# A long convolution and its gradient on one core: from an 8-point-by-channel spectrum with complex products to real products on 4-channel blocks summed in PSUM

## The chip, the core and the metric

The kernel runs on one core of one Trainium2 chip. The metric is the device time of one execution in microseconds. The core's engines have short names in the profile: PE is TensorE's matmul, PEld its weight load, DVE is VectorE, ACT is ScalarE, POOL is GpSimd, SP is SyncE, which here only issues DMAs.

## The reference: what is computed

One block is run forward and backward. The block has two branches on the layernorm of A_q (2,048 tokens by 512 channels, bf16): a gated MLP, and a product with a causal convolution over the whole sequence, which the reference computes by real FFTs of length 4,096.

```
xn = layernorm(A_q)
kv = shift4(A_k) * A_v                       # a 4-tap causal filter, then v
y  = irfft(rfft(kv, 4096) * rfft(ssm_k, 4096))[:2048] + kv * ssm_D
s  = xn * y
g  = silu( (sigmoid(xn @ w_gate) * (xn @ w_up)) @ w_down )
out = A_q + s * g
```

The kernel returns `out` and the gradients of a scalar through it with respect to q, k, v, the shift filter, ssm_k (512 by 2,048), ssm_D and the three MLP weights. The gradient of the convolution needs the spectrum of the gradient dy, and two products of it with a conjugated spectrum: with K's for d(kv), and with kv's for d(ssm_k). Both are transformed back.

## The kernel before: how the work is staged

**Recording and planning.** The kernel doesn't write its instructions in the order in which they run. All of them are recorded in `Rec` (`add`, L234), with their dependencies by region of SBUF or PSUM bank. Generators (strK, strV, strX and so on) are interleaved by `run_streams` (L497), by how much TensorE work each has yielded. `Rec.order` (L337) then plays the list through with a cost for each instruction (`cost` L283, `dcost` L312 for DMAs) and decides in which order each engine gets its instructions, which PSUM bank a tile has, and, for an evacuation recorded by `evac` (L231), whether ScalarE or VectorE does it. `emit` (L487) writes them in this order, so that every compute instruction in the profile stands at L493. An engine takes its instructions strictly in that order, and so does each DMA queue: what waits holds up what is behind it.

**PSUM.** Eight banks are given out by kind (L175): three pairs ("mm2") for the transforms in the first part and two pairs ("mm2c") in the last, two single banks for accumulations ("acc") and two for transposes ("tr"). A matmul group can begin only when a bank of its kind has been evacuated.

**Stage A, to about 182 us: the forward convolution, with part of the MLP beside it.** The 512 channels go in four groups (cg) of 128. The sequence of 2,048 is 128 by 16 (token = 16 p + j). For each group and each of K (the convolution kernel), V (that is, kv) and later C (dy):

- `step1` (L833): 32 matmuls against the cosine and sine tables Cf, one for each j and for real and imaginary part, give Q; four evacuations of 1,024 columns.
- `flip` (L844): 32 transposes, so that the 16 values of j come onto the partitions; four evacuations. A block has 8 channels: 16 j by 8 channels are 128 partitions, and real and imaginary part are separate blocks.
- `step3` (L853), four times a group (qq): the 16-point factor on j. As real and imaginary input are separate blocks, a complex result takes four matmuls of 512 columns, two each into the real and the imaginary half; one evacuation.
- `cmul` (L864): the complex product on VectorE, two multiplications of 1,024 columns and two sums of 512.
- `inv3` (L872): back from the product, eight matmuls of 256 columns (four blocks, each with real and imaginary part), one evacuation.
- `inv1` (L881): the inverse of step1.

`strK` (L892) and `strV` (L914) bring K and V to the flipped form, `strX` (L947) runs step3 for K and V, stores both spectra to HBM as `KK_d` (by POOL's queue) and does the product and the inverse. Beside them runs strG, the MLP's forward pass for ten of the sixteen token blocks (`f_gen`, L687), which has three sigmoids a block on ScalarE. At the very start `gen_fft_consts` (L523) makes the tables: integer angles on VectorE, sines on ScalarE, then BD (the 16-point factor, used by step3) and R (its inverse, used by inv3). The transposes of strK (L900) read their columns with a step of 16 elements.

**Stage B, about 182 to 336 us.** The rest of the MLP forward and its backward, block by block (`stepB`, L1113), with activations transposed by DMA on SP's queue and stored.

**Stage C, from about 336 us: the convolution's gradient beside the weight gradients.** `dW` (L1169) multiplies stored activations, which SP's queue loads (`ld_L`, L1158), into the three weight gradients. Beside it, `frontC` (L1207) brings dy to the flipped form and `backC` (L1229) runs, for each quarter qq of a group: step3, two complex products with the stored spectra (loaded by `ld_KK`, L1201, on POOL's queue into a ring of two), and two inv3, one for each product. The rest of backC gives d(k), d(v), the shift filter's gradient and d(ssm_k). When it has ended, the last weight gradients run alone.

Of the kernel before, what the change touches and what calls it, by code (L numbers as in the profile page):

```python
# [16 lines left out]
P = 128  # L17
# [6 lines left out]
NJ = 16  # L24
# [13 lines left out]
FBS = [(0, 4), (4, 4), (8, 3)]  # L38

# [129 lines left out]
class Rec:  # L169
# [142 lines left out]
    def dcost(self, alt):  # L312
# [17 lines left out]
        rate = 360e3 if run >= 2048 else 300e3 if run >= 1024 else 250e3 if run >= 512 else 150e3 if run >= 256 else run * 500  # L330
# [192 lines left out]
def gen_fft_consts(nc, ar, a, b, negpi, Cf, BD, R):  # L523
# [10 lines left out]
    pa = tmp([1], i32)  # L534
    nc.vector.tensor_single_scalar(pa, pi_, 3, ALU.arith_shift_right)
    pe = tmp([1], i32)
    nc.vector.tensor_single_scalar(pe, pi_, 7, ALU.bitwise_and)
    paf = tmp([1], f32)
    nc.vector.tensor_copy(paf, pa)
    pef = tmp([1], f32)  # L540
    nc.vector.tensor_copy(pef, pe)
    cb = tmp([16, 8], f32)
    nc.gpsimd.iota(cb, pattern=[[1, 16], [0, 8]], base=0, channel_multiplier=0, allow_small_or_imprecise_dtypes=True)
    ce = tmp([16, 8], f32)
    nc.gpsimd.iota(ce, pattern=[[0, 16], [1, 8]], base=0, channel_multiplier=0, allow_small_or_imprecise_dtypes=True)
    ab = tmp([16, 8], i32)
    nc.vector.tensor_scalar(ab, cb, paf[:, 0:1], None, ALU.mult)
    mask = tmp([16, 8], f32)
    nc.vector.tensor_scalar(mask, ce, pef[:, 0:1], None, ALU.is_equal)
    ang = tmp([3, 16, 8], i32)  # L550
    nc.vector.tensor_single_scalar(ang[:, 0], ab, 12, ALU.add)
    nc.vector.tensor_single_scalar(ang[:, 1], ab, 8, ALU.add)
    nc.vector.tensor_copy(ang[:, 2], ab)
    nc.vector.tensor_single_scalar(ang, ang, 15, ALU.bitwise_and)
    angf = tmp([3, 16, 8], f32)
# [11 lines left out]
    tri = tmp([3, 16, 8], f32)  # L567
    nc.scalar.activation(tri, angf, ACT.Sin, bias=negpi, scale=2 * math.pi / 16)
    nc.vector.tensor_tensor(tri, tri, mask[:, None, :, :].to_broadcast([P, 3, 16, 8]), ALU.mult)
    nc.vector.tensor_copy(BD, tri.rearrange("p t b e -> p t (b e)"))  # L570
    for c, ci, t in ((0, 0, 0), (0, 1, 1), (1, 0, 2), (1, 1, 0)):
        nc.vector.tensor_scalar(R[:, c, :, :, ci], tri[:, t], SCALE_INV, None, ALU.mult)
# [9 lines left out]
def kernel_impl(ctx, tc, A_q, A_k, A_v, A_shift_k, A_ssm_k, A_ssm_D, B_x, B_w_gate, B_w_up, B_w_down,  # L582
# [8 lines left out]
    KK_d = dram.tile([NG, 4, 2, P, 2, 512], bf16, name="KK_d")  # L591
# [24 lines left out]
    BD = Ring(ar, [3, 128]).ap  # L616
    R = Ring(ar, [2, 16, 8, 2]).ap
# [116 lines left out]
    QgK_r = Ring(ar, [2, GG, NJ, 8])  # L734
# [5 lines left out]
    QgV_r = Ring(ar, [2, GG, NJ, 8])  # L740
# [76 lines left out]
    QfK_r, QfV_r = Ring(ar, [2, GG, 128], n=2), Ring(ar, [2, GG, 128])  # L817
    KFg_r = Ring(ar, [2, GG, 128])
    Bg_r = Ring(ar, [NJ, GG, 8, 2])
    Xc_r = Ring(ar, [2, 512], n=2)  # L820
    Yc_r = Ring(ar, [2, 512], n=2)
    t2_r = Ring(ar, [2, 512], n=2)
# [10 lines left out]
    def step1(src, Qg):  # L833
        for jb in range(2):
            for c in range(2):
                ps = ps_mm([8, GW], name="ps_q")
                for jj in range(8):
                    j = jb * 8 + jj
                    nc.tensor.matmul(ps[:, jj, :], Cf[:, c, j, :], src(j), start=True, stop=True)
                nc.evac(Qg[:, c, :, jb * 8:(jb + 1) * 8, :].rearrange("p g j e -> p j g e"),  # L840
                         ps[:].rearrange("p j (g e) -> p j g e", e=8), 1024)
                yield 1024

    def flip(Qg, Qf):  # L844
        for gb in range(GG // 8):
            for c in range(2):
                pt = ps_tr([8, 128], name="ps_fl")
                for gi in range(8):
                    nc.tensor.transpose(pt[:, gi, :], Qg[:, c, gb * 8 + gi].rearrange("p j e -> p (j e)"), ident)
                nc.evac(Qf[:, c, gb * 8:(gb + 1) * 8, :], pt[:], 1024)  # L850
                yield 1024
# [573 lines left out]
```

## Time and profile before

| | |
|---|---|
| median of 4 runs | 570.47 us (564.70 to 575.13) |
| the profiled execution | 564.70 us, of which the span of the core's instructions is 562.9 us |
| TensorE clock granted | 1.00 throughout |
| busy: PE, DVE, ACT, POOL | 536.3, 420.7, 342.7, 156.0 us |
| matmuls of 128, 256, 352, 512 columns | 3,652, 384, 128, 1,141 recorded |
| evacuations of 1,024 fp32 on ACT | 154, 1.03 us each |
| loads of KK_d | 16 of 512 KB, 5.6 us from issue to landing |

In a line of groups stand the line of the kernel, the engine, the operation, what it writes and reads (partitions x elements and type), its count, its busy time and the mean ns of one, and the idle time just before it with what ended it. In a timeline's line stand the start and the length in us, then the same, and in brackets an idle time and its end. In a line of waits: who waited for whom, us in total, how many times, the longest. In a line by stage: the stretch, its length, then for PE, PEld, DVE, ACT and POOL the busy us and the count, then the granted clock, the busy share of the DMA engines and GB/s. A busy PE is not a PE at its peak, since matmuls overlap; the distance between the starts of two that follow each other says more.

### The profile page before, as it was taken

What the parts mean: (1) busy time and instruction counts of PE and PEld (TensorE: products, weight loads), DVE (VectorE), ACT (ScalarE), POOL (GpSimd) and SP (SyncE); (2) the same over time, 40 slices, a digit from 0 to 9 for tenths busy, and PEclk for the clock granted to TensorE, in tenths of its full rate; (3) what the DMA queues carried; (4) which work ended last, traced back from release to release, by engine and by line L of the source; (5) the groups of instructions that cost most, each with busy time, mean ns of one, the idle gap of its engine ahead of it and who ended that gap; (6) DMA issues with size and microseconds to landing.
All of it is one profiled execution on the core that took longest, in us unless ns stands there. A gap on an engine that the chain in (4) does not pass through costs nothing.

```text
span 562.9 us, 13136 instructions
## 1 busy us (share of the span) xinstructions
PE 536.3 (95%) x5330; PEld 378.4 (67%) x5389; DVE 420.7 (75%) x873; ACT 342.7 (61%) x454; POOL 156.0 (28%) x266
## 2 busy tenths in 40 slices
PE   3999889999989999999999999999999999999996
PEld 2889678898768566776666765656756666565643
DVE  7589899947777998989898999436478487397350
ACT  7989999977986235444344543467758576345421
POOL 3135225303312222312231212313322522331212
PEclk9999999999999999999999999999999999999999
DMA  8898988675522999997979999999487598575433
GB/s 252 238 251 236 316 210 256 218 188 176 176 73 74 209 200 244 256 250 199 227 199 285 230 193 290 258 279 243 146 259 239 170 320 236 155 236 185 150 121 110
DMA packets 127367, 120.34 MB, mean 214 GB/s; under 512 B 74995, under 2 KB 107593, under 8 KB 127306
## 3 DMA queue, kind: packets, MB, share of 16 engines
q1 hardware_dynamic: 109722, 62.84, 46.4%
q0 software_dynamic: 17056, 56.66, 32.1%
q8 instruction: 42, 0.69, 0.5%
q14 instruction: 19, 0.16, 0.1%
q10 hardware_dynamic: 528, 0.00, 0.0%
HBM read 54.23 MB, written 47.55 MB: 181 GB/s over the span
## 4 chain that ended last, share of the span: by engine, by line
PE 72%; issue 9%; DVE 8%; ACT 7%; POOL 2%; DMA 1%; POOLq 0%; ACTq 0%; DVEq 0%
PE psum L493 72%; DVE slab L493 8%; ACT slab L493 7%; DMA hF_d<-slab 1%; POOL out_dram L493 1%; POOL slab L493 1%; POOL KK_d L493 0%; POOLq L1420 0%; POOL ksh_d L493 0%; POOL sF_d L493 0%; POOL hF_d L493 0%; POOLq L493 0%; ACTq L493 0%; DVEq L493 0%; POOLq L1409 0%
## 5 line engine op out<-in xcount | busy, mean ns | idle before, releaser
L493 PE MATMUL psum<-slab 128*128 128x128 bf16 (+4 forms) x5330 | 536.3, 261 | 21.3 <-ACT slab L493 13.2
L493 PEld LDWEIGHTS <-slab 128*128 128x128 bf16 (+1 forms) x5389 | 378.4, 99 | 178.8 <-issue 13.1
L493 DVE TENSOR_TENSOR slab<-slab 128x512 bf16<-128x512 bf16 (+3 forms) x555 | 291.6, 581 | 38.1 <-ACT slab L493 30.4
L493 ACT CAST slab<-psum 128x1024 bf16<-128x1024 f32 (+3 forms) x242 | 200.0, 858 | 97.8 <-PE psum L493 92.2
L493 ACT COPY slab<-psum 128x1024 bf16<-128x1024 bf16 (+2 forms) x94 | 79.4, 888 | 88.4 <-PE psum L493 86.3
L493 POOL DMA_DIRECT2D out_dram<-slab x75 | 45.3, 605 | 153.7 <-ACT slab L493 82.1
L493 DVE TENSOR_TENSOR slab<-psum,slab 128x512 bf16<-128x512 f32 (+2 forms) x68 | 44.4, 653 | 33.7 <-PE psum L493 24.9
L493 ACT ACTIVATE slab<-slab 128x512 bf16<-128x512 bf16 (+3 forms) x51 | 41.2, 809 | 18.4 <-DVE slab L493 17.9
L493 ACT ACTIVATE slab<-psum 128x512 bf16<-128x512 f32 (+1 forms) x64 | 37.8, 590 | 9.6 <-PE psum L493 8.1
L493 DVE SCALAR_TENSOR_TENSOR slab<-slab 128x1 f32<-128x1 f32 (+3 forms) x64 | 28.0, 438 | 13.8 <-ACT slab L493 12.6
L493 POOL DMA_DIRECT2D KK_d<-slab x32 | 20.0, 628 | 62.7 <-ACT slab L493 53.5
L493 DVE COPY slab<-psum 128x1024 bf16<-128x1024 bf16 (+2 forms) x22 | 14.0, 646 | 19.8 <-PE psum L493 18.3
L493 POOL DMA_DIRECT2D slab<-in_A_q_dram x29 | 16.3, 562 | 36.0 <-DMA out_dram<-slab 27.2
L493 DVE CAST slab<-psum 128x1024 bf16<-128x1024 f32 (+1 forms) x15 | 17.4, 1161 | 9.2 <-PE psum L493 9.0
L493 POOL DMA_DIRECT2D slab<-KK_d x16 | 11.6, 726 | 26.7 <-DVE slab L493 26.6
L493 DVE TENSOR_SCALAR slab<-slab 128x1 f32<-128x1 f32 (+8 forms) x49 | 16.6, 356 | 2.0 <-ACT slab L493 1.8
L493 POOL DMA_DIRECT2D slab<-in_grad_out_dram x16 | 8.7, 541 | 29.8 <-DMA out_dram<-slab 23.2
L493 POOL TENSOR_TENSOR slab<-slab 128x1 f32<-128x1 f32 x16 | 11.5, 721 | 18.5 <-DVE slab L493 18.3
L493 DVE SCALAR_TENSOR_TENSOR slab<-psum,slab 128x512 f32<-128x512 f32 x16 | 11.0, 684 | 6.8 <-PE psum L493 6.7
L493 POOL DMA_DIRECT2D slab<-slab x8 | 4.5, 567 | 24.7 <-issue 17.0
L493 POOL DMA_DIRECT2D slab<-in_A_k_dram x12 | 10.1, 845 | 2.9 <-PE psum L493 1.7
L493 DVE BATCH_NORM_STATS2 slab<-slab 128x6 f32<-128x512 bf16 x16 | 10.9, 684 | 0.0
(22 smaller groups left out, 44.5 us busy)
## 6 DMA issues: line engine op xcount, KB each, us to landing
KK_d<-slab POOLq DMA_DIRECT2D x32, 256.0 KB, 3.2
slab<-KK_d POOLq DMA_DIRECT2D x16, 512.0 KB, 5.6
out_dram<-slab POOLq DMA_DIRECT2D x58, 128.0 KB, 4.3
hS_d<-slab SPq DMA_DIRECT2D x16, 352.0 KB, 3.5
dgS_d<-slab SPq DMA_DIRECT2D x16, 352.0 KB, 4.5
duS_d<-slab SPq DMA_DIRECT2D x16, 352.0 KB, 4.1
slab<-hS_d SPq DMA_DIRECT2D x8, 512.0 KB, 5.4
slab<-dgS_d SPq DMA_DIRECT2D x8, 512.0 KB, 5.3
```

The costliest lines, as they stand in the source:

```text
L493: getattr(getattr(self.nc, eng), meth)(*[place(v) for v in a], **{x: place(v) for x, v in k.items()})
```

## The change

**Blocks.** A block of the transform has 4 channels instead of 8, and holds real and imaginary part together: 2 by 16 j by 4 channels are 128 partitions. `GQ = 32` such blocks make a group of 128 channels. One matmul of 512 columns thus gives a complex result for four blocks. Q lies as (c, j, e, g), so that the columns which flip transposes are 32 elements (64 bytes) apart, where they lay side by side before; what step1's evacuation writes is now contiguous, and what it reads from PSUM has a step of four elements.

**Both orders.** A real elementwise product of (re, im) with a spectrum gives only half of a complex product; the other half needs the spectrum in the order (im, re). step3 therefore has two tables: X_RI gives (re, im), X_IR gives (im, re). K needs only the first (two matmuls a quarter), V and C run both (two each). Each order is evacuated by itself. `cmul` is gone: a product is two multiplications of 1,024 columns with no sums. The sums and signs are made by `inv3`, which multiplies both product parts by tables of their own (R_A and R_B forward, R_C and R_D for the conjugate) and adds them in PSUM: sixteen matmuls of 128 columns.

**Constants.** The tables need eight sections of angles instead of three, each of 64 columns, some with an offset by partition.

**Loads and rings.** A quarter of KK_d is contiguous for a partition (4 KB). Its load goes to SP's queue, the ring has four buffers, and a load is asked for three quarters ahead. In C the multiplications with the (re, im) order overwrite the loaded KK. frontC runs step1 before it waits and has one Qf instead of two. The planner's DMA rate for long runs is 340 for 360 and 290 for 300 GB/s.

```diff
+SECS = [(12, -4), (0, 12), (12, -8), (8, -8), (0, 0), (12, 0), (8, 0), (0, 8)]
+X_RI, X_IR = range(2)
+BDSEC = [(0, 1), (1, 0)]
+R_A, R_B, R_C, R_D = range(4)
+RSEC = [(2, 3), (4, 5), (5, 6), (7, 2)]
...
-        rate = 360e3 if run >= 2048 else 300e3 if run >= 1024 else 250e3 if run >= 512 else 150e3 if run >= 256 else run * 500
+        rate = 340e3 if run >= 2048 else 290e3 if run >= 1024 else 250e3 if run >= 512 else 150e3 if run >= 256 else run * 500
...
-    ab = tmp([16, 8], i32)
-    nc.vector.tensor_scalar(ab, cb, paf[:, 0:1], None, ALU.mult)
...
-    ang = tmp([3, 16, 8], i32)
-    nc.vector.tensor_single_scalar(ang[:, 0], ab, 12, ALU.add)
-    nc.vector.tensor_single_scalar(ang[:, 1], ab, 8, ALU.add)
-    nc.vector.tensor_copy(ang[:, 2], ab)
+    dc = {0: None}
+    for d in (-4, 12, -8, 8):
+        dc[d] = tmp([1], f32)
+        nc.vector.tensor_single_scalar(dc[d], pf[:, 0:1], float(d), ALU.mult)
...
+    ang = tmp([NSEC, 16, 4], i32)
+    for n, (off, d) in enumerate(SECS):
+        if d:
+            nc.vector.tensor_scalar(ang[:, n], ab, dc[d][:, 0:1], float(off), ALU.add, ALU.add)
+        else:
+            nc.vector.tensor_single_scalar(ang[:, n], ab, float(off), ALU.add)
...
-                nc.evac(Qg[:, c, :, jb * 8:(jb + 1) * 8, :].rearrange("p g j e -> p j g e"),
-                         ps[:].rearrange("p j (g e) -> p j g e", e=8), 1024)
+                nc.evac(Qg[:, c, jb * 8:(jb + 1) * 8], ps[:].rearrange("p j (g e) -> p j e g", e=4), 1024)
...
-                    nc.tensor.transpose(pt[:, gi, :], Qg[:, c, gb * 8 + gi].rearrange("p j e -> p (j e)"), ident)
-                nc.evac(Qf[:, c, gb * 8:(gb + 1) * 8, :], pt[:], 1024)
+                nc.tensor.transpose(pt[:, gi, :], Qg.rearrange("p c j e g -> p (c j e) g")[:, :, g], ident)
+            nc.evac(Qf[:, gb * 8:(gb + 1) * 8, :], pt[:], 1024)
...
-    def step3(Qf, qq, dst):
-        qre = Qf[:, 0, 4 * qq:4 * qq + 4, :].rearrange("p g k -> p (g k)")
-        qim = Qf[:, 1, 4 * qq:4 * qq + 4, :].rearrange("p g k -> p (g k)")
+    def step3(Qf, qq, which, dst):
         ps = ps_mm([2, 512], name="ps_x")
-        nc.tensor.matmul(ps[:, 0], BD[:, 0, :], qre, start=True, stop=False)
-        nc.tensor.matmul(ps[:, 0], BD[:, 1, :], qim, start=False, stop=True)
-        nc.tensor.matmul(ps[:, 1], BD[:, 2, :], qre, start=True, stop=False)
-        nc.tensor.matmul(ps[:, 1], BD[:, 0, :], qim, start=False, stop=True)
-        nc.evac(dst, ps[:], 1024)
-        yield 2048
+        lhs = BD[:, which].rearrange("p c j e -> p (c j e)")
+        for h in range(2):
+            nc.tensor.matmul(ps[:, h], lhs, Qf[:, 8 * qq + 4 * h:8 * qq + 4 * h + 4, :].rearrange("p g k -> p (g k)"),
+                             start=True, stop=True)
+        nc.evac(dst, ps[:].rearrange("p h x -> p (h x)"), 1024)
+        yield 1024
...
-    def inv3(Y, qq, Bg):
-        ps = ps_mm([4, NJ, 16], name="ps_b")
-        for gg in range(4):
-            for c in range(2):
-                nc.tensor.matmul(ps[:, gg].rearrange("p j x -> p (j x)"), Y[:, c, gg * 128:(gg + 1) * 128],
-                                 R[:, c].rearrange("p j e c -> p (j e c)"), start=(c == 0), stop=(c == 1))
+    def inv3(terms, qq, Bg):
+        ps = ps_mm([8, NJ, 8], name="ps_b")
+        for g in range(8):
+            for n, (Y, r) in enumerate(terms):
+                nc.tensor.matmul(ps[:, g].rearrange("p j x -> p (j x)"), Y[:, g * 128:(g + 1) * 128],
+                                 R[:, r].rearrange("p j e c -> p (j e c)"), start=(n == 0), stop=(n == len(terms) - 1))
...
                 if qq < 4:
-                    Xc = Xc_r.next()
-                    yield from step3(QfV, qq, Xc)
-                    nc.gpsimd.dma_start(KK_d[cg, qq, 1], Xc)
-                    ys[qq] = Yc_r.next()
-                    cmul(Xc, KFg[:, :, 4 * qq:4 * qq + 4, :].rearrange("p c g k -> p c (g k)"), ys[qq], False)
+                    Xc, Xs, Y = Xc_r.next(), Xs_r.next(), Y_r.next()
+                    yield from step3(QfV, qq, X_RI, Xc)
+                    nc.gpsimd.dma_start(KK_d[cg, qq, :, 1], Xc)
+                    nc.vector.tensor_tensor(Y, Xc, KFg[:, qq], ALU.mult)
+                    yield from step3(QfV, qq, X_IR, Xs)
+                    nc.vector.tensor_tensor(Xs, Xs, KFg[:, qq], ALU.mult)
+                    ys[qq] = ((Y, R_A), (Xs, R_B))
...
-            nc.gpsimd.dma_start(KK, KK_d[n // 4, n % 4].rearrange("t p c x -> p t c x"))
+            nc.sync.dma_start(KK, KK_d[n // 4, n % 4])
...
-            while cg > 1 and ("s3C", cg - 2) not in flags:
-                yield 0
             Qg = Qg_r.next()
             yield from step1(lambda j: y2A[:, j, cg * GW:(cg + 1) * GW], Qg)
+            while cg > 0 and ("s3C", cg - 1) not in flags:
+                yield 0
...
-                    Xc = Xc_r.next()
-                    yield from step3(Qf, qq, Xc)
+                    Xr, Xi = Xr_r.next(), Xi_r.next()
+                    yield from step3(Qf, qq, X_RI, Xr)
+                    yield from step3(Qf, qq, X_IR, Xi)
...
-                    Y1, Y2 = Y1_r.next(), Y2_r.next()
-                    cmul(Xc, KK[:, 0], Y1, True)
-                    cmul(Xc, KK[:, 1], Y2, True)
-                    ys[qq] = (Y1, Y2)
+                    ys[qq] = KK, T2_r.next()
+                    for t in range(2):
+                        nc.vector.tensor_tensor(ys[qq][1][:, t], KK[:, t], Xi, ALU.mult)
+                        nc.vector.tensor_tensor(KK[:, t], KK[:, t], Xr, ALU.mult)
...
-                    Y1, Y2 = ys.pop(qq - 1)
-                    yield from inv3(Y1, qq - 1, B1)
-                    ld_KK(cg * 4 + qq + 1)
-                    yield from inv3(Y2, qq - 1, B2)
+                    T1, T2 = ys.pop(qq - 1)
+                    for t, B in ((0, B1), (1, B2)):
+                        yield from inv3(((T1[:, t], R_C), (T2[:, t], R_D)), qq - 1, B)
+                    ld_KK(cg * 4 + qq + 3)
...
-    KK_r = Ring(ar, [2, 2, 512], n=2)
+    KK_r = Ring(ar, [2, 1024], n=4)
-    Qf_r = Ring(ar, [2, GG, 128], n=2)
+    Qf_r = Ring(ar, [GQ, 128])
```

## The prediction

> **What bounds the kernel now.** I read the page first, then the busy time by stage, the waits of TensorE, the groups by shape and two stretches of the timeline. Columns of the stages: busy us and count of PE, PEld, DVE, ACT, POOL, then clock, DMA share, GB/s.
>
> ```profile
> PE 536.3 (95%) x5330; PEld 378.4 (67%) x5389; DVE 420.7 (75%) x873; ACT 342.7 (61%) x454; POOL 156.0 (28%) x266
> PE 72%; issue 9%; DVE 8%; ACT 7%; POOL 2%; DMA 1%; POOLq 0%; ACTq 0%; DVEq 0%
> ```
> ```profile
> 0.00:21.60 21.60, 12.92 (x140) 10.99 (x141) 15.83 (x41) 16.32 (x17) 4.60 (x16) 1.00 0.98 273
> 21.60:62.80 41.20, 39.40 (x617) 35.88 (x617) 34.59 (x62) 37.20 (x50) 16.36 (x28) 1.00 0.85 238
> 62.80:98.80 36.00, 31.79 (x422) 26.92 (x425) 34.29 (x56) 34.43 (x45) 13.69 (x21) 1.00 0.91 255
> 98.80:134.10 35.30, 34.99 (x502) 30.98 (x504) 22.98 (x40) 30.23 (x39) 8.81 (x16) 1.00 0.71 201
> 134.10:182.00 47.90, 45.07 (x533) 35.81 (x537) 36.72 (x71) 38.56 (x50) 11.90 (x21) 1.00 0.36 115
> 182.00:336.00 154.00, 152.41 (x1501) 102.54 (x1513) 140.72 (x363) 65.98 (x114) 37.41 (x67) 1.00 0.96 225
> 336.00:512.00 176.00, 174.34 (x1341) 109.39 (x1363) 117.25 (x217) 105.11 (x125) 52.72 (x81) 1.00 0.84 240
> ```
> ```profile
> PE psum L493 <- ACT slab L493: 7.4, 12, 1.9
> ```
> The reader is to see that TensorE carries the chain (72%) and that from 182 us on it is idle for 1.6 of 154 and 1.7 of 176 us: there only TensorE's own work counts. Up to 182 us, the forward convolution (stage A), it is otherwise. Between 62.8 and 98.8 us ScalarE and VectorE are both 95% busy and TensorE idles 4.2 us; the waits of TensorE between 20 and 190 us (third fence) are for ScalarE's evacuations. A busy TensorE says little about its pace, as matmuls overlap: in the trace, starts follow each other by 56, 109 and 216 ns at 128, 256 and 512 columns. These are the prices.
>
> ```profile
> L493 PE MATMUL psum<-slab 128*128 128x512 bf16 x1141 | 272.1, 379 | 5.5 <-ACT slab L493 1.8 <-DVE slab L493 0.8 <-issue 0.2
> L493 PE MATMUL psum<-slab 128*128 128x256 bf16 x384 | 52.1, 272 | 3.4 <-ACT slab L493 2.9 <-DVE slab L493 0.3
> L493 ACT CAST slab<-psum 128x1024 bf16<-128x1024 f32 x154 | 154.1, 1032 | 44.9 <-PE psum L493 43.4 <-ACT slab L493 1.2
> L493 DVE TENSOR_TENSOR slab<-slab 128x512 bf16<-128x512 bf16 x320 | 119.9, 417 | 1.0
> L493 DVE TENSOR_TENSOR slab<-slab 128x1024 bf16<-128x1024 bf16 x96 | 62.3, 686 | 17.5 <-ACT slab L493 15.0 <-DMA slab<-KK_d 2.3
> ```
> An evacuation of 1,024 fp32 costs ScalarE 1.03 us (VectorE 1.22, by its own row of that answer), a complex product's halves VectorE 0.42 and 0.69.
>
> [...] the kernel transposes with a step of 16 elements (32 bytes) in strK, and the weight loads of such a batch (first line, eight of nine) take 1.5 times those with short steps (second line).
>
> ```profile
> L493 PEld LDWEIGHTS <-slab 128*128 128x128 bf16 x9 | 0.6, 144 | 0.0
> L493 PEld LDWEIGHTS <-slab 128*128 128x128 bf16 x73 | 4.5, 97 | 0.7
> ```
> Their matmuls start 62 ns apart, not 56.
>
> **The change, part by part.** The sum is against the profiled execution (564.7 us: span 562.9 and 1.8 around it), which is 5.8 us below the median 570.47; I carry the difference over.
>
> TensorE. (1) K's spectrum: 16 calls of step3 go from four 512-column matmuls to two: −32 × 216 ns = −6.9 us, all in stage A. V's and the gradient's 16 calls each become two of two: nothing. (2) inv3, 16 calls in A and 32 in the backward stage C: eight matmuls of 256 become sixteen of 128, 16×56 − 8×109 = +24 ns a call: +0.4 and +0.8. (3) flip: as many transposes (256 in A, 128 in C), now with weights 64 bytes apart. No row shows 64; below, the 56 ns of short steps; above, as an outer mark, the 107 ns at which they start in the first 16 us of this trace. I take 62, [...]: +6 ns × 384, +1.5 in A and +0.8 in C. TensorE in all: A −5.0, C +1.6.
>
> VectorE and ScalarE. The 512-column sums of the products go: −32 × 0.417 = −13.3 us of VectorE in A, −26.7 in C; the 1,024-column products stay 32 and 64. Each second order is one more evacuation: +16 in A and +16 in C. In C VectorE (117 of 176 us) and ScalarE (105) have room, and what hides them is the weight-gradient matmuls; I price both at 0 there. If that cover fails, 16 × 1.03 us are late, and a PSUM slot with each. In A what counts is where the planner puts them, and the listing of both orders shows it. Between the first and the thirtieth sigmoid of the gate (21.6 to 134.1 us) ScalarE gets 87 evacuations for 82 and VectorE 19 for 13, against 18 sums less (−7.5 us): ScalarE rises, VectorE stays. ScalarE's 101.9 busy us there (37.20 + 34.43 + 30.23, of 112.5) become 107. The densest stretch ran it at 34.43/36.00 = 95.6%; at this density 107 needs 111.9 us: −0.6. Bounds: −4.5 (all of TensorE's saving in this stretch) and +5.6 (ScalarE's mean density, 90.6%).
>
> 134 to 182 us: V's last groups with little other work. Product to inverse was a row of four VectorE operations (2×0.69 + 2×0.42 = 2.2 us) and is one of 0.69 behind each evacuation. TensorE idles 2.8 us here; I take back 1.0 (0 to 2.8).
>
> Start. Two waits decide here:
> ```profile
> 7.28 2.00 ACT L493 ACTIVATE slab<-slab 128x2048 bf16<-128x2048 int32 x1 [1.16 <-DVE slab L493]
> 9.32 0.70 DVE L493 TENSOR_SCALAR slab<-slab 128x1024 int32<-128x1024 int32 x1 [1.80 <-ACT slab L493]
> ...
> 10.38 0.81 ACT L493 ACTIVATE slab<-slab 128x512 bf16<-128x512 bf16 x1 [1.10 <-DVE slab L493]
> ```
> VectorE's fourth 1,024-wide angle operation waits until ScalarE's first sine is done (second line). In the old order the first token's layernorm statistics are ahead of it, in the new one behind it, with five 1-wide, eight 64-wide and a 1,024-wide operation on top; on ScalarE the second sine now goes ahead of the layernorm. Worked through with the durations above, the sine starts at 6.1 (it is freed from the angles earlier, then by the table load that ends there) and ends at 8.1, the statistics end at 10, POOL's power (1.08) at 11, the second sine at 13.2, the layernorm at 14.0 instead of 11.2, and VectorE's addition to K, for which the next transposes wait, at 14.5 instead of 12.2. TensorE does eight turns of constants (8×0.107 us) in between: +1.2 us (0 to +2.5).
>
> Queues. The 16 loads of KK leave POOL (0.73 us of issue each) for SP, where weight-gradient loads wait for TensorE, 25.8 us the longest, and hold up what is behind. KK is now four deep and asked for three quarters ahead; sixteen quarters took 338 to 508 us, 10.6 each, so 32 us stand against 25.8 + 5.6 of landing: nothing, but narrow; if late, VectorE's products and then the inverse wait. frontC holds one Qf instead of two, so a group's flip waits for the step3 of the group before; inverse and diagonal matmuls and the weight gradients cover the two evacuation times: nothing. POOL's stores stay 32. The planner's DMA rate moves orders only: nothing.
>
> Sum: −0.6 (to 134 us) − 1.0 (to 182) + 1.2 (start) + 1.6 (C) = +1.2 us, 565.9 for such an execution, 571.7 as a median.
>
> **Rivals.** (a) TensorE's saving lands: −4.5 − 2.8 + 1.6 and an unharmed start, −5.7 us: 564.8. For it: TensorE is 99% busy from 99 to 134 us. Against: the stretch before. (b) Evacuation binds all of A: +5.6 + 2.5 + 1.6 = +9.7: 580. For it: both other engines at 95%; against: VectorE has 12 free us from 99 to 134. (c) Slower: weights 64 bytes apart load more slowly than at 32. It decides from 2% (11.4 us) on, 10.2 beyond my sum, 27 ns on each of 384 transposes: starts 89 ns apart. At 107, 45 × 384 = +17.3: 589. For it: no such step is in the trace; [...]. (d) Faster by over 2%: the forty us taken from VectorE remove TensorE's waits in A altogether (TensorE idles 9.2 us from 21.6 to 182), and its saving comes on top: −5.0 − 9.2 + 1.6 = −12.6: 558. Against: ScalarE ends most of these waits, and gains work. (e) That the change doesn't do what it says: excluded for K's matmuls, as the order has 32 fewer of 512 columns.
>
> **How the numbers follow.** Main case 0.43, (a) 0.24, (b) 0.17, (c) 0.10, (d) 0.06. About 2% is what a measurement of this kernel can tell from no change. Faster by over 2%: (d) and 0.02 of (a), 0.08. Slower: (c) and 0.04 of (b), 0.14. Within: 0.78. The range 562 to 583 holds the main case, (a) and most of (b), and leaves (d), (c) and the end of (b) out.
>
> **What would show it.** 128-column matmuls +768, 256-column ones gone, 1,172 of 512; flip's weight loads near 148 ns, which rules (c) out, near 100 or over 200, which would make me wrong; ScalarE above 95% from some 60 to 100 us with TensorE waiting for it (a and d fall); dense matmuls from about 14 us; no TensorE wait on KK after 340 us. A stage C that grows by more than 3 us would make the cover of its evacuations wrong.

## The result, and the profile after

The changed kernel takes 571.03 us in the median (43 runs, 569.57 to 578.59), the kernel before 569.16 (64 runs, 564.03 to 575.13). The ratio is 1.0051 with a 95% interval of 1.0034 to 1.0068: slower by 2.9 us (1.9 to 3.9), clear of noise but only 0.5%. The forecast was 571.7.

The profiled execution of after took 571.28 us with a span of 569.5, close to its median. The profiled one of before, with its span of 562.9, was at the fast end of its runs. The two profiles are thus 6.6 us apart where the medians are 1.9 apart, and this has to be kept in mind at every line below.

Busy time and chain of after, from its page:

```profile
PE 536.3 (94%) x5681; PEld 385.4 (68%) x5741; DVE 409.1 (72%) x812; ACT 357.6 (63%) x468; POOL 140.6 (25%) x250
PE 69%; DVE 8%; ACT 8%; issue 8%; DMA 4%; POOL 2%; POOLq 0%; SPq 0%; DVEq 0%; ACTq 0%
```
ScalarE has 15 us more and VectorE 12 less; a DMA has come into the chain (4% for 1%). The stages of after, cut at the first, 14th, 21st, 30th, 36th and 63rd sigmoid on ScalarE (counted are its activations that read PSUM; columns as in the prediction). The 36th lies near the beginning of stage B, the 63rd just ahead of stage C:

```profile
22.20:65.20 43.00, 39.48 (x635) 37.09 (x634) 35.36 (x62) 38.15 (x51) 15.94 (x27) 1.00 0.75 189
65.20:106.90 41.70, 34.35 (x477) 29.42 (x483) 36.59 (x55) 40.19 (x50) 12.36 (x22) 1.00 0.88 265
106.90:141.90 35.00, 34.74 (x539) 32.10 (x542) 26.62 (x36) 30.90 (x40) 8.31 (x16) 1.00 0.76 200
141.91:194.72 52.81, 49.83 (x599) 38.22 (x606) 41.48 (x80) 39.97 (x52) 13.19 (x24) 1.00 0.44 127
194.72:337.98 143.26, 141.74 (x1407) 95.66 (x1417) 130.02 (x336) 61.32 (x107) 34.64 (x63) 1.00 1.04 222
337.98:569.49 231.51, 224.77 (x1937) 143.37 (x1963) 124.63 (x194) 130.05 (x158) 51.66 (x83) 1.00 0.72 214
```
From the 14th to the 21st sigmoid 36.0 us have become 41.7, with ScalarE busy for 40.19 of them. The last three stretches took 55.8, 143.3 and 229.7 us before: the stretch with the end of stage A is 3.0 shorter, stage B as it was, and what follows, stage C, 1.8 longer. (The first sigmoid comes at 22.2. In before it is the one at 19.3 us; the 21.6 of the prediction is the second. So the start is 2.9 us longer, and the stretch to the 14th, from 19.3, was 43.5 long and is 43.0.) The waits of TensorE between 20 and 190 us:

```profile
PE psum L501 <- ACT slab L501: 10.0, 20, 1.2
PE psum L501 <- DVE slab L501: 2.3, 7, 0.5
```
12.3 us in all. Before there were 7.4 for ScalarE (the prediction's third fence) and 0.4 for VectorE:

```profile
PE psum L493 <- DVE slab L493: 0.4, 2, 0.3
```
So the evacuations hold TensorE longer than before, by 4.5 us. Groups by shape:

```profile
L501 PE MATMUL psum<-slab 128*128 128x128 bf16 x4420 | 279.4, 221 | 19.0 <-ACT slab L501 13.1 <-DVE slab L501 4.7
L501 PE MATMUL psum<-slab 128*128 128x512 bf16 x1108 | 263.7, 379 | 7.2 <-ACT slab L501 2.3 <-DVE slab L501 1.9 <-issue 0.4
L501 ACT CAST slab<-psum 128x1024 bf16<-128x1024 f32 x172 | 170.1, 1030 | 35.5 <-PE psum L501 33.8 <-DVE slab L501 0.9 <-ACT slab L501 0.3
```
There are 768 matmuls of 128 columns more and those of 256 are gone, as forecast. The 33 records of 512 columns fewer are K's 32 matmuls and one more record missing than before. Some records of 512 columns are missing in both: the fuller traces of the two kernels with plain copies, below, have 1,200 and 1,168 of them, which is nearer to the prediction's 1,172. 18 evacuations came to ScalarE at the same 1.03 us.

### The profile page after: what moved, and what is told of

It is laid out like the page before. It is cut to its first block, busy times and chain, and to the rows that moved or that the text cites. A ratio compares the mean times of both kernels' runs of the same rounds, so it can differ in the third digit from the quotient of the medians.

```text
span 569.5 us, 13831 instructions
## 1 busy us (share of the span) xinstructions
PE 536.3 (94%) x5681; PEld 385.4 (68%) x5741; DVE 409.1 (72%) x812; ACT 357.6 (63%) x468; POOL 140.6 (25%) x250
## 4 chain that ended last, share of the span: by engine, by line
PE 69%; DVE 8%; ACT 8%; issue 8%; DMA 4%; POOL 2%; POOLq 0%; SPq 0%; DVEq 0%; ACTq 0%
PE psum L501 69%; DVE slab L501 8%; ACT slab L501 8%; DMA slab<-in_A_k_dram 3%; POOL out_dram L501 1%; DMA ksh_d<-slab 1%; DMA hF_d<-slab 1%; DMA slab<-in_A_shift_k_dram 0%; ACT L501 0%; POOL KK_d L501 0%; POOL slab L501 0%; POOL sF_d L501 0%; POOLq L1422 0%; SPq L501 0%; POOLq L501 0%
## 5 line engine op out<-in xcount | busy, mean ns | idle before, releaser
L501 PEld LDWEIGHTS <-slab 128*128 128x128 bf16 (+1 forms) x5741 | 385.4, 102 | 179.2 <-issue 24.0
L501 DVE TENSOR_TENSOR slab<-slab 128x512 bf16<-128x512 bf16 (+4 forms) x459 | 259.2, 615 | 34.1 <-ACT slab L501 25.8
L501 ACT CAST slab<-psum 128x1024 bf16<-128x1024 f32 (+4 forms) x259 | 214.8, 868 | 85.0 <-PE psum L501 73.8
L501 ACT ACTIVATE slab<-slab 128x512 bf16<-128x512 bf16 (+2 forms) x51 | 41.0, 807 | 18.1 <-DVE slab L501 17.7
L501 DVE CAST slab<-psum 128x1024 bf16<-128x1024 f32 (+1 forms) x30 | 35.5, 1185 | 14.0 <-PE psum L501 13.7
L501 DVE COPY slab<-psum 128x1024 bf16<-128x1024 bf16 (+2 forms) x25 | 15.2, 618 | 30.1 <-PE psum L501 30.0
L501 DVE SCALAR_TENSOR_TENSOR slab<-slab 128x1 f32<-128x1 f32 (+3 forms) x64 | 28.0, 438 | 11.8 <-ACT slab L501 10.8
L501 POOL DMA_DIRECT2D KK_d<-slab x32 | 17.5, 548 | 65.5 <-ACT slab L501 54.2
L501 DVE TENSOR_SCALAR slab<-slab 128x1 f32<-128x1 f32 (+6 forms) x65 | 18.0, 313 | 3.6 <-ACT slab L501 2.1
L501 POOL TENSOR_TENSOR slab<-slab 128x1 f32<-128x1 f32 x16 | 10.8, 676 | 27.6 <-DVE slab L501 27.4
L501 DVE BATCH_NORM_STATS2 slab<-slab 128x6 f32<-128x512 bf16 x16 | 10.8, 682 | 0.0
L501 POOL MEMSET slab<- 1x384 bf16 (+4 forms) x14 | 5.7, 418 | 13.2 <-DVE slab L501 8.4
```

The lines of the kernel that those rows point to most:

```text
L501: getattr(getattr(self.nc, eng), meth)(*[place(v) for v in a], **{x: place(v) for x, v in k.items()})
```

## The experiments

Ratios are always to the kernel before, with their 95% intervals. As its runs spread over 11 us, a ratio is uncertain by 2 to 3 per mille; where the runs of an experiment and of its control each lie within some 2 us, their medians say more. In the profiles, the sigmoids are the marks.

In the profiles of before and after, ScalarE ran its copies and activations (451 and 465) and SP's queue issued its DMAs (158 and 174) exactly in the order that `emit` wrote. An edit that changes what the planner sees also changes that order. By the traces, ScalarE, VectorE and GpSimd have the order of the control in the two kernels with the start's wait alone taken out, in those with plain copies alone, and in that with less traffic. In the others it parts from the control's: with contiguous weights at 147 us, with K's matmuls twice at 28, with evacuations left out at 65, with the other price for ScalarE and with the old rates at 14, with the small operations moved at 4. There the effect of the work and that of the order come together.

**The start.** The edit gives each half of the angles a buffer of its own. Every engine keeps its order; one wait goes.

```diff
-    mc = tmp([2, 16, 128], i32)
+    mch = [tmp([2, 8, 128], i32) for _ in range(2)]
     for h in range(2):
+        mc = mch[h]
```


> Changed kernel, with a buffer of its own for each half of the table angles, so that VectorE's fourth 1,024-wide operation no longer waits for ScalarE's first sine; the order on every engine is unchanged. Theory (the start costs about 2.9 us, of which this wait is part): that operation starts at about 6.3 us instead of 8.4, but ScalarE's sine itself starts no earlier, so VectorE's later operations gain up to 2 us; the first sigmoid comes at about 20.5 to 21 us instead of 22.2, and the whole is 1.0 to 1.7 us shorter than the changed kernel: ratio to before about 1.0025. Rival (the loss arises from 60 to 107 us, the start only shifts slack): first sigmoid earlier, the end not: 1.005.

Measured: 569.26 us, 1.0009 (0.9979 to 1.0039), 1.8 us less than the changed kernel by the medians and 2.4 by the ratios. The first sigmoid comes at 19.8. The mark comes earlier than expected, and the whole gains more. So what the start loses is lost at the end too; it is no slack. The waits at issue are these, from the timeline of after:

```profile
6.33 2.00 ACT L501 ACTIVATE slab<-slab 128x2048 bf16<-128x2048 int32 x1
8.36 0.69 DVE L501 TENSOR_SCALAR slab<-slab 128x1024 int32<-128x1024 int32 x1 [2.06 <-ACT slab L501]
11.12 3.32 ACT L501 ACTIVATE slab<-slab 128x2048 bf16<-128x2048 int32 x3 [2.79 <-DVE slab L501]
```
VectorE waits 2.06 us for the sine, and ScalarE then 2.79 us for VectorE, which has the end of the statistics, small operations and the last angles to do first. With the edit the first of these waits is gone, and the second sine starts at 8.97. The three operations of the last line are the second sine, the layernorm and the sections' sine, in the order that the prediction worked out.

**Flip with contiguous weights.**

```diff
-  nc.evac(Qg[:, c, jb * 8:(jb + 1) * 8], ps[:].rearrange("p j (g e) -> p j e g", e=4), 1024)
+  nc.evac(Qg[:, :, c, jb * 8:(jb + 1) * 8], ps[:].rearrange("p j (g e) -> p g j e", e=4), 1024)
...
-  nc.tensor.transpose(pt[:, gi, :], Qg.rearrange("p c j e g -> p (c j e) g")[:, :, g], ident)
+  nc.tensor.transpose(pt[:, gi, :], Qg[:, g].rearrange("p c j e -> p (c j e)"), ident)
```


> Changed kernel, with Q laid out by block, so that flip's weights lie side by side again (step 1 instead of 32 elements) and the evacuation of step1 writes runs of four elements instead. Theory: weight loads of the flips fall from about 148 to 98 ns, the starts of these matmuls from 62 to 56 ns apart; this counts only where TensorE is dense (stage C, 128 transposes: -0.8 us) and is swallowed by ScalarE's pace in stage A: ratio about 1.004. Rival 1 (TensorE sets the pace everywhere): 384 x 6 ns = -2.3 us, 1.001. Rival 2 (scattered writes slow the evacuation): CAST of 128x1024 above 1.05 us on ScalarE and a ratio above 1.005.

Measured: 571.79 us, 1.0049 (1.0025 to 1.0072): no gain on the whole. In the profiles the time from the 63rd sigmoid to the end falls from 231.5 to 230.6, which is stage C's share as expected (0.8), but the 52.8 us from the 30th to the 36th become 54.8, where the order is another. Evacuations stay at 1,030 ns, which excludes rival 2. Rival 1's 2.3 us are not there.

**K's matmuls twice.**

```diff
-        for h in range(2):
+        for h in (0, 0, 1, 1) if twice else (0, 1):
             nc.tensor.matmul(ps[:, h], lhs, ...
```
Only K's calls of step3 set `twice`.

> Changed kernel, with each of the two matmuls of K's spectrum done twice into the same place (32 matmuls of 512 columns more, all in stage A, 6.9 us of TensorE at 216 ns; the result is the same). This undoes the saving of TensorE alone. Theory (ScalarE's evacuations bind most of stage A to 107 us, TensorE the rest): between +2 and +4 us on the changed kernel, ratio 1.009 to 1.012. Rival 1 (TensorE sets the pace all through): the full +6.9 us, 1.017. Rival 2 (stage A is bound by evacuations all through, TensorE's saving was worth nothing): within 1 us, 1.005 to 1.007.

Measured: 574.18 us (six runs, 572.72 to 580.86), 1.0119 (1.0058 to 1.018): 3.2 us of the 6.9 added by the medians, 3.9 by the ratios, as the theory had it, though the interval reaches from near nothing to the full amount. In the profile, the time from the first to the 30th sigmoid grows by 0.6 us only (120.3 for 119.7), although three of the four groups of K lie in it; from the 30th to the 36th, with the fourth, by 2.1 (54.9 for 52.8). But the edit does not undo the saving alone. From the 14th to the 21st sigmoid ScalarE now has 28 evacuations of 1,024 and not 36, and the stretch takes 35.7 us and not 41.7. So what the saving is worth up to the 30th sigmoid is not shown.

**Evacuations left out.**

```diff
-                    yield from step3(QfV, qq, X_IR, Xs)
-                    nc.vector.tensor_tensor(Xs, Xs, KFg[:, qq], ALU.mult)
+                    yield from step3(QfV, qq, X_IR, Xs, False)
+                    nc.vector.tensor_tensor(Xs, Xc, KFg[:, qq], ALU.mult)
```
With False, step3 runs its matmuls and evacuates nothing.

> Changed kernel, leaving out in stage A the evacuation of V's second order (16 of 1,024 columns): its matmuls run, but the second product is taken from the first order, so the forward convolution's values are not the reference's. All else is as it was. Theory (the added evacuations eat TensorE's saving): stage A gets 4 to 6 us shorter, most of it between the 14th and the 21st sigmoid (41.7 us in the changed kernel, 36.0 before) and after the 30th; ratio 0.995 to 0.998. Rival (the stretch is long because the second half of A_k lands at 76 us, late behind a store on SP's queue): that stretch stays within 1 us of 41.7, ratio 1.003 to 1.005.

Measured: 567.06 us, 0.998 (0.9956 to 1.0005), 4.0 us less than the changed kernel. The amount fits the theory, the place doesn't: the stretch from the 14th to the 21st sigmoid is 39.6 us and not 36. It holds another wait, which after has too, from the timeline of after:

```profile
67.64 8.28 SPq L501 DMA_DIRECT2D hS_d<-slab  x1
76.52 5.36 DVE L501 TENSOR_TENSOR slab<-slab 128x2048 bf16<-128x2048 bf16 x5 [2.74 <-DMA slab<-in_A_k_dram]
```
The second half of A_k, issued at 61.3 us, lands at 76.1, and VectorE's filter of the third group waits for it (2.74 us here, 5.6 with the evacuations left out). A store holds SP's queue for 8.28 us behind it. Is this load the cause of the long stretch, or is it the evacuations?

**Copies for transposes: the two controls.** SP's queue and the DMA engines also carry 48 transposing DMAs of stored activations. In the remaining eight kernels they are plain copies of as many bytes, and the planner prices them as before, so that every other instruction keeps its place.

```diff
-  nc.sync.dma_start_transpose(st.rearrange("p (a b) -> p a b", b=128), srcT.rearrange("p a t -> p (a t)"))
+  nc.sync.dma_start(st, srcT.rearrange("p a t -> p (a t)"))
```


> Changed kernel in which the 48 DMAs that transpose activations on SP's queue are plain copies of as many bytes: the stored activations are not transposed, so the three weight gradients are not the reference's. The order on every engine and queue is the same. It is the control for the next kernels, which have the same copies. Expected: if these DMAs hold up nothing, the stage times of the changed kernel (first sigmoid 22.2, 14th to 21st 41.7, 30th at 141.9) within 1 us each, ratio 1.003 to 1.007; if the copies disturb less than transposes, shorter.

> The kernel before with the same plain copies instead of transposing DMAs (weight gradients not the reference's), the control on the other side. Expected: ratio 0.997 to 1.001, the first sigmoid at 19.3, 36.0 us from the 14th to the 21st, and so the same distance to the changed kernel with copies as between the two originals, 0.3 to 0.7%. If that distance is gone, the transposing DMAs have a part in it.

Measured: after with copies 569.27 us (568.08 to 569.66), 1.0017 (0.9996 to 1.0039); before with copies 564.72 (563.94 to 565.41), 0.9946 (0.9926 to 0.9966). The distance does not stay, it grows to 4.5 us by the medians (4.0 by the ratios): the transposing DMAs cost the kernel before 4.4 us in the median (3.1 by the ratio, 1.9 to 4.2) and spread its runs over 11 us, and they cost the changed kernel 1.8 (1.9 by the ratios). With copies the runs of either lie within 1.6 us. Stages of before with copies and, in the second fence, of after with copies (from the first, 14th and 21st sigmoid to the next mark):

```profile
19.43:62.91 43.48, 41.77 (x652) 37.80 (x650) 36.94 (x65) 39.49 (x53) 17.08 (x28) 1.00 0.73 243
62.91:98.86 35.95, 31.96 (x425) 26.93 (x425) 34.28 (x56) 34.38 (x45) 13.65 (x21) 1.00 0.70 251
98.86:134.22 35.36, 35.32 (x508) 31.03 (x506) 23.04 (x40) 30.29 (x40) 8.80 (x16) 1.00 0.56 202
```
```profile
21.84:64.12 42.28, 39.10 (x631) 36.70 (x629) 36.02 (x62) 38.09 (x51) 15.92 (x27) 1.00 0.63 216
64.12:104.16 40.04, 34.15 (x481) 29.39 (x481) 36.51 (x55) 39.81 (x50) 13.05 (x22) 1.00 0.70 254
104.16:139.19 35.03, 35.00 (x543) 32.19 (x542) 26.70 (x36) 30.95 (x40) 8.23 (x16) 1.00 0.56 200
```
The profile of before with copies (span 563.0) is that of before (562.9) mark by mark within 0.1 us: the execution of before that was profiled shows none of the loss of its median. In after with copies A_k lands in 8.4 us instead of 14.8, VectorE's wait is gone, and the stretch is still 40.0 us long. So the late load took at most some 1.7 us of the 5.7. TensorE's waits from 20 to 190 us are 10.8 us here and 7.8 in before with copies. ScalarE is 99% busy (39.81 of 40.04) in what remains.

**Less traffic.** Of each store of h and sigmoid only a block in eleven is moved, when the order has been fixed.

```diff
+                if meth == "dma_start" and str(a[0].space) == "DRAM" and a[0].tensor.name in ("hF_d", "sF_d"):
+                    a = a[0][:, 0:1], a[1][:, 0:1]
```


> Changed kernel with plain copies for transposes, the order on every engine and queue untouched, but of each of the fourteen stores of h and sigmoid for later use (352 KB each, between about 25 and 115 us) only one block in eleven is moved; what stage B reads back is incomplete too, so the MLP's gradients are not the reference's. It takes traffic from the stretch in which the second half of A_k is loaded. Theory A (that load, 14.8 us from issue to landing, holds VectorE and so the forward convolution): it lands in under 10 us, VectorE's wait of 2.7 us is gone, and the stretch between the 14th and 21st sigmoid falls by 3 us or more against the control. Theory B (the stretch is long by its evacuations alone): the load lands earlier, the stretch and the whole stay within 1 us of the control.

Measured: 569.12 us, 1.0006 (0.9989 to 1.0024), the control's time within 0.2 us; the stretch is 40.0, the load lands in 8.0. It comes out as Theory B has it: this traffic does not make the stretch long. Whether the evacuations alone do is another question.

**ScalarE priced at its measured speed.**

```diff
-            c = 0.05 + n / 1200 + ...
+            c = 0.05 + n / 1060 + ...
```


> Changed kernel with plain copies for transposes, in which the planner prices ScalarE at its measured speed (1.02 us for an evacuation of 1,024 instead of 0.90). It hands VectorE seven evacuations more between the 1st and 30th sigmoid (26 instead of 19; ScalarE 80 instead of 87). Theory (ScalarE's evacuations set stage A's pace): 7 x 1.02 us of ScalarE gone at a density of 96% is up to 7 us, of which VectorE's 7 x 1.22 us eat a part where it is busy too: 2 to 4 us shorter than the control, and TensorE's waits for ScalarE between 20 and 190 us fall below 7 us. Rival (the start and the late load make the loss): within 1 us of the control.

Measured: 567.64 us, 1.0000 (0.9977 to 1.0024), 1.6 us less than the control, a little under what the theory gave. TensorE's waits for ScalarE are 7.9 us, not under 7, and for VectorE 2.0 (9.9 and 0.9 in the control). But the gain lies at the start (first sigmoid at 20.8 for 21.8) and from the 30th to the 31st (31.9 for 34.8); 1.5 us of it are lost again behind. From the first to the 21st, for which the edit was made, it takes 83.7 us for 82.3. Three stretches of 1.5 us in it:

```profile
58.50:60.00 1.50, 0.59 (x2) 0.19 (x2) 1.50 (x3) 1.50 (x4) 1.04 (x2) 1.00 0.02 7
60.00:61.50 1.50, 0.59 (x2) 0.19 (x2) 1.50 (x3) 1.50 (x3) 0.29 (x2) 0.93 0.98 204
61.50:63.00 1.50, 0.81 (x2) 0.26 (x2) 1.50 (x3) 1.50 (x2) 1.49 (x2) 0.50 0.84 217
```
VectorE and ScalarE are both full, TensorE has two matmuls in each, and the granted clock, the third value from the end, falls to 0.50 in the second stretch and stays there until about 68 us. TensorE was never idle for longer than 1.2 us at a time; of these 4.5 us it worked for 2.0. What tipped the clock is not shown. So behind the jam of evacuations came some 7 us at half the clock, and this stretch says nothing clean about ScalarE's share. The mean clock was 0.994 to 0.996 in all runs of this kernel.

**Evacuations left out, with copies.** The edit is that of the earlier run.

> Changed kernel with plain copies for transposes, leaving out in stage A the evacuation of V's second order as well (16 of 1,024 columns; the matmuls run, the second product is taken from the first order, so the forward convolution is not the reference's). Control: 569.3 us, 40.1 us from the 14th to the 21st sigmoid, 34.8 from the 30th to the 31st. In the earlier run of this kind the late load of A_k held VectorE 5.6 us; with copies it should not. Theory (from the 1st to the 21st sigmoid the evacuations and vector work of ScalarE and VectorE together set the pace; eight evacuations more than in the kernel before are there): the 1st-to-21st stretch falls from 82.4 to 78 to 79.5, and the whole by 4.5 to 6 us, to 563.3 to 564.8. Rival (the order, not the amount of work, makes that stretch longer): it stays above 81 and the whole falls by 2 to 3.5 us.

Measured: 566.28 us, 0.9971 (0.9951 to 0.9992), 3.0 us less than the control; 81.7 us from the first to the 21st sigmoid. The rival holds: seven evacuations fewer there than in the control (63 for 70), and 0.6 us. The two stretches up to the 21st sigmoid:

```profile
21.71:64.80 43.09, 39.95 (x639) 37.41 (x639) 36.23 (x63) 38.95 (x52) 15.94 (x27) 1.00 0.65 222
64.80:103.45 38.65, 34.11 (x464) 30.11 (x470) 32.95 (x51) 35.69 (x45) 12.81 (x22) 0.96 0.69 253
```
The clock was at 0.96 in the second, but the five runs of this kernel in which it stayed at 1.00 were only some 0.5 us shorter than the others. The amount of work alone does not make the stretch long.

**The start in the kernel before.** The edit is that of the first experiment.

> The kernel before with plain copies for transposes, and a buffer for each half of the table angles, so that VectorE's fourth 1,024-wide operation doesn't wait for ScalarE's first sine. Control: 564.7 us, first sigmoid at 19.4. Theory (in the old order the layernorm statistics stood ahead of that wait, so it held up little): the first sigmoid comes at most 0.8 us earlier and the whole is 0 to 0.8 us shorter. Rival (the wait costs the same in both kernels, and is no part of the change's loss): 2 to 2.5 us shorter, as the changed kernel was.

Measured: 563.26 us (562.9 to 563.57), 0.9906 (0.9879 to 0.9932), 1.5 us less than before with copies by the medians (2.3 by the ratios), and the first sigmoid at 18.1 for 19.4. By the medians that is between the two expectations, by the ratios the rival's: of the 1.8 to 2.4 us that this wait costs the changed kernel, more than half it cost before too.

**The start, and the small operations behind the large.** The same buffers, and the loop over the two halves is recorded ahead of the block that makes the sections' angles:

```diff
+    m = tmp([16, 128], i32)
+    mch = [tmp([2, 8, 128], i32) for _ in range(2)]
+    for h in range(2):
...
     pq, pf = tmp([3], i32), tmp([3], f32)
...
     nc.vector.tensor_copy(angf, ang)
-    m = tmp([16, 128], i32)
-    mc = tmp([2, 16, 128], i32)
-    for h in range(2):
...
```


> Changed kernel with plain copies for transposes, with a buffer for each half of the table angles, and with the small sections' angles recorded behind the large ones, so that the layernorm statistics and the second half of the angles go ahead of them on VectorE. Control: 569.3 us, first sigmoid at 21.8. Theory (the start costs 2.4 us because VectorE is held and then has twenty small operations in front of the second sine): first sigmoid at 19.0 to 19.8, the whole 2 to 3 us shorter, 566.3 to 567.3. Rival (only the wait counts, and what is gained at the start is lost between the 1st and 21st sigmoid): first sigmoid as above, the whole within 1 us of the control.

Measured: 564.62 us, 0.9940 (0.9917 to 0.9963), 4.7 us less than the control (4.4 by the ratios). That is more than the theory allows. The first sigmoid comes at 19.9 (-1.9); the other 2 us come from between the first and 30th sigmoid, 115.4 us for 117.4. But the same work is in it: 88 evacuations of 1,024 on ScalarE and 19 on VectorE for the control's 87 and 19. The edit of the constants shifted the planner's order all the way down. So the order itself is worth 2 us in this stretch, at the new rates. Which edit of the change made it?

**The planner's rates.** One line of the diff, priced at nothing, is taken back alone:

```diff
-        rate = 340e3 if run >= 2048 else 290e3 if run >= 1024 else ...
+        rate = 360e3 if run >= 2048 else 300e3 if run >= 1024 else ...
```


> Changed kernel with plain copies for transposes, and the planner's two DMA rates back at 360 and 300 GB/s, as before the change. Only the planned order differs: from the 1st to the 30th sigmoid ScalarE has 87 and VectorE 19 evacuations of 1,024 in both, between the 14th and the 21st ScalarE 33 instead of 36. Control: 569.3 us, 1st to 21st sigmoid 82.4, 1st to 30th 117.4. Theory (the order, not the amount, made this stretch longer, and the rates are one of the edits that set it): the 1st-to-30th stretch moves by more than 1 us with the same work, to 115 to 116.5 if the new rates are what lengthened it, and the whole with it. Rival (the rates cost nothing, as priced; the product's new form alone gave the order): stretch and whole within 1 us of the control.

Measured: 565.01 us (564.71 to 566.35), 0.9941 (0.9916 to 0.9965): 4.3 us less than the control, more than the theory gave. With the old rates the changed kernel with copies stands at the time of the kernel before with copies (564.72). Its stages at the same three marks:

```profile
21.18:65.87 44.69, 39.91 (x627) 36.91 (x628) 39.24 (x67) 39.16 (x52) 17.79 (x30) 1.00 0.64 218
65.87:101.04 35.17, 32.92 (x486) 29.43 (x488) 33.02 (x51) 35.17 (x45) 9.58 (x17) 1.00 0.75 273
101.04:136.61 35.57, 35.14 (x536) 32.11 (x538) 24.66 (x38) 32.61 (x43) 8.91 (x17) 1.00 0.54 193
```
ScalarE is full in the middle stretch here too (35.17 of 35.17). But from the first to the 21st sigmoid it has 74.3 us of work where the control has 77.9 (38.09 + 39.81), and 1.7 us more in the following stretch, where it has room (32.61 of 35.57). Read so, the new rates pulled evacuations forward into the one stretch without room. That is argued from the profiles and not shown: with the evacuations left out ScalarE has as little to do there (38.95 + 35.69 = 74.6 us), and the time is 81.7 us, against 79.9 here and 82.3 in the control. The rest came from the start (0.7 us: VectorE takes one more of K's first evacuations there) and from 1.0 us after the 30th sigmoid. TensorE's waits from 20 to 190 us are 8.9 us, for 10.8. With the transposing DMAs in place the old rates were not measured.

## Why the forecast held, and which of its steps failed

The number held, its working only in part. For the profiled kind of execution I had worked out 565.9 us; it took 571.28, 5.4 more. I then added the 5.8 us between the profile of before and its median; the median of after, 571.03, is not above its profile at all. The two errors cancelled, which was luck. The gap of 5.8 us rested on four runs (with 64 it is 4.5) and belonged to the kernel before, most of it to its transposing DMAs (3.1 to 4.4 us, for 1.8 in after). How they lose it there, and why less in after, stays open: no execution of before that had the loss was profiled. The clock goes with it: of 67 executions of before in one series, the 27 with a mean granted clock of 0.996 or less took 568.8 to 573.5 us, the 34 with 0.998 or more 563.9 to 569.3. Whether that is cause or effect isn't shown.

The step that failed is the one on queues, as it was put: **"The planner's DMA rate moves orders only: nothing."** It moves orders only, and this costs 4.3 of the 4.5 us by which the change is slower without the transposing DMAs. It is this one order that is dear, and not the rates as such: another order at the new rates, that with the small operations moved, gave back 2 us too. Everything else together is +0.3 us (565.01 for 564.72), against a forecast of +1.2. By terms, from the sigmoids of before and of after with copies and the old rates. The last stretches of the two, from the 30th to the 36th sigmoid and from the 63rd to the end, are these:

```profile
134.20:189.99 55.79, 53.28 (x587) 39.80 (x585) 44.58 (x93) 40.48 (x53) 13.47 (x24) 1.00 0.38 134
333.25:562.98 229.73, 223.99 (x1710) 138.10 (x1707) 138.58 (x250) 122.80 (x150) 63.64 (x99) 1.00 0.65 209
```
```profile
136.58:188.77 52.19, 49.12 (x592) 37.77 (x600) 43.51 (x80) 39.52 (x51) 13.37 (x25) 1.00 0.40 144
332.01:563.27 231.26, 224.62 (x1936) 143.57 (x1963) 124.03 (x193) 131.17 (x159) 51.44 (x83) 1.00 0.65 207
```

- **To 134 us, -0.6 forecast.** From the first to the 30th sigmoid 114.8 became 115.4: +0.6. The amount of ScalarE's work was right: 104.2 us busy from the first sigmoid on, and five evacuations more would give 109.3; it is 109.2 in after. The density was not. I took the 95.6% of the densest stretch for the whole; it came to 92.6% with the old rates (106.9 of 115.4) and to 91.3% in after. Of the bounds, the upper one, which used the mean density, was nearer to after: 119.7 for 114.8, +4.9 against +5.6; with copies, without the late load, it is +2.6 (117.4), halfway between the forecast and that bound.
- **134 to 182 us, -1.0.** From the 30th to the 36th sigmoid 55.8 became 52.2: -3.6, and 52.9 with the new rates, -2.9. Both are beyond the range of 0 to 2.8 that the prediction gave. It took back a part of TensorE's idle time, but that stayed (2.5 us, now 3.1); what fell is TensorE's work, 53.3 to 49.1 us. By the counts of before and after with copies, 8 matmuls of 512 columns are gone there (87 for 95), K's last group: 1.7 us at 216 ns. Of 128 columns there are 522 for 428, though inv3 alone should add 128: some 30 of them, about 1.8 us at 56 ns, now stand ahead of the 30th sigmoid, a shift between this term and the first.
- **Start, +1.2.** First sigmoid 19.4 to 21.2: +1.8, and +2.4 with the new rates. The mechanism was right: the end of the statistics behind the fourth angle operation, the small operations, the second sine (it ended at 13.1, I had 13.2), then the layernorm; VectorE's addition to K came at 13.65, where I had 14.5. The size was low because of what followed. ScalarE has six evacuations of 1,024 ahead of the first sigmoid in after, five with the old rates and three before, and VectorE two, three and four; I hadn't counted them here.
- **Stage C, +1.6.** From the 63rd sigmoid to the end 229.7 became 231.3: +1.5, and +1.9 with the new rates (231.6). Right. The cover of the 16 evacuations held, and the flip's part was as priced (0.8): 0.9 us are gained there with contiguous weights.
- **K's matmuls, -6.9 us of TensorE.** There, and about half hidden: put back, in an order that moved with them, they cost 3.2 to 3.9 us on the whole, 0.6 from the first to the 30th sigmoid and 2.1 from there to the 36th.

Of the rivals, (c) falls. The 62 ns for a flip's matmul was my estimate: no row of before showed weights 64 bytes apart, and I put them at the pace of those 32 bytes apart. They load no more slowly, here eight loads of a flip of after in stage C:

```profile
L501 PEld LDWEIGHTS <-slab 128*128 128x128 bf16 x8 | 0.6, 147 | 0.1
```
They take 147 ns in the mean, those at 32 bytes 144 (the nine loads of before in the prediction): no cost of the wider step shows. (a) and (d) fall, since TensorE waits more for evacuations (12.3 for 7.8 us); but behind the 30th sigmoid (a)'s -2.8 was nearer than the forecast. (b) came nearest in its mechanism up to there, but with the old rates it costs 0.6 us and not 5.6. None of the rivals had the order in it.

The KK loads on SP's queue were narrow and held: TensorE waits for none of them after 340 us.

## What to carry to other kernels

Where an order is planned ahead, a constant of the planner's model is part of the change, with a price of its own: take it back alone before explaining the rest. In a stretch where two engines are both nearly full, the amount of work alone doesn't set the time (74.6 and 74.3 us of ScalarE's work stood in 81.7 and 79.9 us); where the planner puts it matters too, and the density of the best place is not to be had everywhere. An experiment that changes the work also gets a new order, so compare the orders before reading its time. Cut the stages of both profiles at marks of the program: only so does it show that the end of stage A gained 3 us and stage C lost 1.8. And before carrying the gap between a profile and a median over to a new kernel, find out what makes the gap.

## What was not expected of the hardware

- Plain copies for 48 transposing DMAs of 352 KB took 3 to 4.4 us off the kernel before, and its spread with them: 564.03 to 575.13 us became 563.94 to 565.41. The late load of A_k landed in 8.4 us instead of 14.8 in the changed kernel, but in 9.1 instead of 7.8 (its last piece, of 22.5 KB) in the kernel before, so its lateness isn't put down to them.
- An evacuation that reads PSUM with a step of four fp32 costs ScalarE what a contiguous one does: 1,030 ns is the mean of after's 172, 1,032 that of before's 154. About a quarter of after's read with the step (48 of 200 on both engines, step1's), none of before's. The 39 of these on ScalarE take 1,025 ns in the mean, its other 133 take 1,031.
- With the other price for ScalarE, TensorE's clock fell to 0.50 from about 61 to 68 us, in and after a stretch in which evacuations let it work for 2.0 of 4.5 us, without an idle time over 1.2 us.
